# Attention with two key tiles of sixteen as one float, and turning products in the bank of the P V sums

## The chip, the cores and the metric

The kernel runs on one core of a Trainium2 chip. The core has five engines that run their own instruction streams and wait for each other by semaphores: TensorE (PE in the profile; PEld are its weight loads), VectorE (DVE), ScalarE (ACT), GpSimd (POOL) and SyncE (SP), which here only starts DMA transfers. Matrix products land in PSUM, which has eight banks of 128 partitions x 512 floats. The metric is the device time of one execution in microseconds.

## The reference

One transformer block with modulation from a condition vector. The input is 2048 rows of 512 floats. First `h = layernorm(x) * (1 + ca) + sa`, then attention with 32 heads of 16 columns each, and `x + ga * attention(h)`; then a second layernorm with modulation and a mixer block (shifted GELU columns, two more products of 512 x 512, and an MLP of width 1792). The part that the change touches is the attention:

```python
scores = jnp.einsum("bhqd,bhkd->bhqk", q, k) * (Dh ** -0.5)
p = _softmax(scores, axis=-1)
o = jnp.einsum("bhqk,bhkd->bhqd", p, v)
```

All of it is in fp32, and the kernel keeps near-fp32 accuracy by splitting operands into a high and a low part.

## The kernel before

The attention is cut into 64 units: 4 chunks of 512 queries (`ci`) times 16 pairs of heads (`pr`). The two heads of a pair sit in partitions 0 to 63 and 64 to 127. A unit has 16 steps, one for each tile of 128 keys; a step `s` is unit `s // 16`, key tile `s % 16`, and there are 1024 steps.

For each step and head, TensorE makes the transposed scores of 128 keys x 512 queries (`sc`, L1026) and, for a unit 24 steps ahead, a tile of scores the other way round (`mb`, L999), of which VectorE takes the row maximum (`mx`, L995). The maxima of a unit are negated and written by eight small DMAs into extra rows of the query operand (`qtl<-nm`), so that the scores arrive with the maximum subtracted. A score product and a maximum product use the two halves of TensorE's rows and run side by side; the two together are called a row pair here.

ScalarE takes the exponential of `sc` and writes it as a 32-bit integer with 26 binary places into a tile of P (`pt` or `xbs`, L1022), two heads side by side. The upper 16 bits of each integer, read as fp16, are the high part of P. The lower 16 bits must be converted to fp16 first: one instruction of 128 x 1024 elements for each step, on GpSimd (L1075) or, when GpSimd is behind, on ScalarE (L1073, shown as a helper's line L158 in the profile's rows).

P V is then summed in one bank of PSUM (`pv`) by columns. A high column (L1100) is four products of 32 output rows, two per head, and serves one step. A low column (L1097) is again four products and serves two steps. V is stored as three bf16 pieces, a column of a constant that gives the softmax sum, and an fp16 copy for the low column. The four products of a column use four column strips of TensorE.

At a unit's end ScalarE copies the sums (`ac`, L1117), and four fp32 products with a constant matrix turn them and add the three pieces (`ot`, L1127). These are called turning products here. ScalarE copies the result (`sm`, L1134), VectorE takes reciprocals (`rc`, L1142) and GpSimd scales into the output (`osb`, L1138).

The order of all instructions is made by the program itself when it is built. A small planner (`Sched`) keeps a planned time for each engine. The main loop goes through blocks of three row pairs. For each block it emits the row pairs, the conversions of earlier steps and then the P V columns that are due by a list of gates (`pvs`), and the other engines' work follows by planned costs (CROW 232, CCOL 240 ns and so on). Of the eight banks one is the bank of the P V sums, and seven are shared by `sc`, `mb` and all other products (`NSM`). The turning products take one of these seven and are slipped in by a generator (`o_fin`) when a bank and time are free. TensorE, like each engine, works strictly through its own list.

While query chunk 0 runs, the remaining projections of Q, K and V are slipped in between the blocks. After that the attention runs alone, and near its end the first part of the mixer begins (`tail(0)`, 30 steps before the end); the other three parts of the mixer follow after the attention. The weights of the mixer come as 1 MB pieces (`wr<-Ws`). The first three are started 140 steps before the attention's end, with a planned pause of 3 us after each, and then four row blocks of x are loaded from ScalarE's DMA queue (L1295). K and Q of a unit (`kst<-Ks`, `qtl<-Qs`) are loaded two units ahead and V (`vst<-Vs`) six steps ahead, all from SyncE's queue.

P lies in six tiles of a pool and, from step 264 on, in two more that use a buffer of the mixer (`xbs`); a low column is delayed by up to three half steps (`LOWLAG`).

Of the kernel before, what the change touches and what calls it, by code (L numbers as in the profile page):

```python
# [83 lines left out]
XBF = 4  # L84
XBT = 4
T0S = 30
T0L = 140
T0W = 3000.0
RATE3 = 1000.0
BURST3 = 1300.0  # L90
BF, BR = 2, 3
# [14 lines left out]
LNG = (1, 3)  # L106
LNC = 2
VP = 2
WIDE = range(S // CH * 64 + 8, 984)
LOWLAG = 3  # L110
XB = 4


# [219 lines left out]
def kernel(ctx, tc, A_x, A_wqkv, A_wo, B_w1, B_w2, B_w3, B_w4, c, w_mod, out):  # L333
# [93 lines left out]
    def dbank(n):  # L427
        return sch.take(lambda i: psd["d"].tile([P, CH], F32, name=n, tag=f"s{i}" if psd["s"] else f"d{i}", bufs=1))
# [540 lines left out]
            load_rows(kst[u % 3], j, Ks, h, slice(0, S), slice(0, S))  # L969

    def load_v(u):
        vst[u] = at.tile([P, NKT, 192], BF16, name="vst", tag="vst", bufs=2)
        sch.dma(dma.dma_start, vst[u], Vs[units[u][1]])

    sm = Slots(NSM)
    ptx = []
    e_exp, e_hi, e_low, v_free, acs = {}, {}, {}, [0.0], []

    def bank(nm):
# [23 lines left out]
    def new_pt(s):  # L1003
        if s in WIDE:
            i = pn[0] % (NPT + len(ptx)) - NPT
            pn[0] += 1
            if i >= 0:
                pt[s] = ptx[i]
                return
        pt[s] = at.tile([P, 2, CH], I32, name="pt", tag="pt", bufs=NPT)  # L1010

    def score_part(s, j):

        u, kt = divmod(s, NKT)
        if j == 0:
            new_pt(s)
        x, b = bank("sc")
        ready, sm.t[x] = sm.t[x], LATE
        r = slice(64 * j, 64 * j + 64)

        def after(e):
            ea = sch.crit("A", 480, e + PX, lambda: act.activation(pt[s][:, j], b, AF.Exp))  # L1022
            sm.t[x] = ea + XP["A"]
            if j:
                e_exp[s] = e_hi[s] = ea
        return ready, lambda: te.matmul(b, kst[u % 3][r, kt * P:(kt + 1) * P], qst[u][r], start=True, stop=True), after  # L1026

    def row_pair(s, j):
# [33 lines left out]
    def p_low(s):  # L1062
# [11 lines left out]
        else:  # L1074
            e_low[s] = XP["G"] + sch.crit("G", 1345, ready, lambda: pool.tensor_scalar(  # L1075
                o, i, 0.5, 1.0, op0=OP.mult, op1=OP.mult))

    def pv_ready(s, lo):

        return max(e_low[s], e_low[s + 1]) if lo else max(e_hi.pop(s), v_free[0] if s % NKT == 0 else 0.0)  # L1080

    def pv_part(s, lo):
# [27 lines left out]
    def ac_copy():  # L1110
        u, e = acs.pop()
        while u and ("ot", u - 1) not in done:
            sch.step()
        ac = at.tile([P, CH], F32, name="ac", tag="ac", bufs=1)
        vst.pop(u)
        acc = pv.pop(u)
        e = sch.crit("A", cA(), e + PX, lambda: act.activation(ac, acc, AF.Copy))  # L1117
        v_free[0] = e + XP["A"]
        sch.add(o_fin(u, ac, e + XP["A"]), 0)

    def o_fin(u, ac, ready):
        ci, pr = units[u]
        yield lambda: sch.T["P"] >= ready and sch.room()
        n = 2 * (DH + 1)
        b = dbank("ot")[:, :TPC * n]
        for t in range(TPC):
            te.matmul(b[:, t * n:(t + 1) * n], ac[:, t * P:(t + 1) * P], smat.rearrange("p j d -> p (j d)"), start=True, stop=True)  # L1127
            yield 110
        done.add(("ot", u))
        sm = at.tile([P, 8, DH + 1], F32, name="sm", tag="sm", bufs=2)  # L1130
        rc = at.tile([P, 8, 1], F32, name="rc", tag="rc", bufs=2)

        def sums():
            act.activation(sm.rearrange("p th d -> p (th d)"), b, AF.Copy)  # L1134
            sch.free(b)

        def fin():
            pool.tensor_tensor(osb[ci][:, :, pr * 32:pr * 32 + 32].rearrange("p t (h d) -> p t h d", d=DH),  # L1138
                              sm[:, :, 0:DH].rearrange("p (t h) d -> p t h d", h=2),
                              rc.rearrange("p (t h) o -> p t h o", h=2).to_broadcast([P, TPC, 2, DH]), op=OP.mult)  # L1140

        sch.chain(("A", 170, sums), ("D", 90, lambda: dve.reciprocal(rc, sm[:, :, DH:DH + 1])), ("G", 350, fin),  # L1142
                  *([mark(("att", ci))] if pr == NP - 1 else []), prio=0, bank=b)


    GW = 130 + CH + 2
# [141 lines left out]
    def tail_loads():  # L1288
        rings["0"] = Ring(FRONT, [], "r")
        for _ in range(BR):  # L1290
            rings["0"].add([("wr", BR)])
            yield sch.wait(T0W)
        for t in range(TPC):
            x1t[t] = fa.tile([P, D], F32, name="x1", tag="x1", bufs=X1F)
            act.dma_start(x1t[t], x_d[t * P:(t + 1) * P])  # L1295

    def tail(ci):
        end = ci == NC - 1
# [147 lines left out]
        def gelu(b, n, hi, lo, key):  # L1446
            me = gn[0]
            gn[0] += 1
            live.append(me)
            sq = fa.tile([P, 3 * P], F32, name="sq", tag="sq", bufs=XB)[:, :n]  # L1450
# [149 lines left out]
    def before(s):  # L1600
# [17 lines left out]
    blocks = [list(range(i, min(i + GRP, 2 * NS))) for i in range(-2 * LEAD, 2 * NS, GRP)]  # L1618
    pvs = []
    for s in range(0, NS, 2):  # L1620
        low = 2 * s + 2 + (min(LOWLAG, 2 * (NKT - 2 - s % NKT)) if s in WIDE else 0)
        pvs += [(2 * s, s, 0), (2 * s + 2, s + 1, 0), (low, s, 1)]
    pvs.sort(key=lambda x: x[0])
    due = 0.0
    for k, blk in enumerate(blocks + [[]] * (LAG + CPER)):
# [13 lines left out]
        if k >= LAG and (k % CPER == 0 or not blk):  # L1639

            x = (blocks[min(k - LAG, len(blocks) - 1)] or [-1])[-1]
            while pvs and pvs[0][0] < x and not (col and pvs[0][1] % NKT == 0 and not pvs[0][2]):
                col.append(pvs.pop(0)[1:])
        t, start = CIN, 0.0
        need = sum((s >= 0) + (s + LEAD < NS) for s, _ in row)
        sch.flush(need)
# [6 lines left out]
            t += CROW  # L1653
        t += CMID
        for s, i in col:
            start = max(start, pv_ready(s, i) - t)
            t += CCOL
        sch.gap(start)
        sch.flush(need)
        sch.T["P"] = max(sch.T["P"], start) + CIN  # L1660
# [8 lines left out]
            p_low(s)  # L1669
        sch.T["P"] += CMID  # L1670
        for s, i in col:
            pv_part(s, i)
        sch.T["P"] += COUT
        for e in "ADG":
            sch.misc(e, max(sch.T["P"], sch.T[e]) + TOLE[e])
        if s0 < 0:
            sch.fill(LEADB / 2 * len(blk))
        elif sch.gens:
# [5 lines left out]
        if 2 * (NS // NC) - 1 in blk:  # L1684
# [8 lines left out]
            fa = o0x.enter_context(tc.tile_pool(name="fa", bufs=1, side="right"))  # L1693
            big = {"A4": fa.tile([P, 4 * KT * 2 * P], F32R, name="A")}
            xbs = fa.tile([P, XBF, D], F32, name="xbs")
            xns = {k: fa.tile([P, XN[k], D], F32, name=k) for k in ("xn", "xf")}
            xnum = {"xn": 0, "xf": 0}
            ptx += [xbs[:, 2 * i:2 * i + 2].bitcast(I32) for i in range(2)]
            big["A"] = big["A4"]
        if blk and blk[0] <= 2 * (NS - T0L) <= blk[-1]:  # L1700
            sch.add(tail_loads())
        if blk and blk[0] <= 2 * (NS - T0S) <= blk[-1]:
            sch.add(tail(0))
    if acs:
# [53 lines left out]
```

## Time and profile before

| | |
|---|---|
| median of 3 runs | 2003.88 us (2003.48 to 2003.94) |
| profiled execution | 2006.74 us, its span 2004.8 us |
| TensorE, weight loads | 1939.3 us, 1161.6 us busy |
| VectorE | 1656.6 us busy (83%) |
| ScalarE | 1519.9 us busy (76%) |
| GpSimd | 1551.9 us busy (77%) |
| first and last copy of P V sums (L1117) | at 167.8 and 1513.7 us |
| row maxima (L995) | 2048, 678 ns mean |
| exponentials (L1022) | 1688 + 360, 623 and 639 ns mean |
| conversions on GpSimd (L1075) | 773 + 165, 1367 and 1363 ns mean |

The time has three stages: up to about 520 us the projections and query chunk 0, to about 1514 us the rest of the attention, and then the mixer. A row of a group gives the line, engine, operation, output and inputs, shapes, the count, busy microseconds and mean nanoseconds of one, and after the second bar the idle time just before them with what ended it. Mean durations overlap for instructions that follow each other in a pipeline, so the distance between starts tells more than a duration. The first numbers of a timeline row are start and length in microseconds.

### The profile page before, as it was taken

Reading aid. Unit: us, or ns where it says so; the run is one execution under the profiler, and the core shown is the slowest. Engines: PE = TensorE matmul, PEld = TensorE weight load, DVE = VectorE, ACT = ScalarE, POOL = GpSimd, SP = SyncE. Lnnn points to the kernel's source line nnn. Section 1 sums busy time; section 2 is a strip of 40 time slices with the busy share of each in tenths; the row PEclk is TensorE's granted clock in tenths of the full one; section 3 lists DMA queues with packets and bytes.
Section 4 is the critical chain, followed back from the end, with each engine's and each line's share of the span. In section 5 each row is a group of like instructions: output and inputs, shape, how many; then the busy total and the mean of one; then the engine's idle time right before and its main releaser. Section 6 shows DMA issues by size and latency. Waiting matters only on the chain.

```text
span 2004.8 us, 41627 instructions
## 1 busy us (share of the span) xinstructions
PE 1939.3 (97%) x14456; PEld 1161.6 (58%) x14456; DVE 1656.6 (83%) x2979; ACT 1519.9 (76%) x3100; POOL 1551.9 (77%) x1473
## 2 busy tenths in 40 slices
PE   7999999999999999999999999999998899999999
PEld 5755554554444444444444444444456788888998
DVE  6398888879999999999999999998976786656443
ACT  6438987768999999999999999998985545344443
POOL 6339998888999999999999999998995564435222
PEclk9989999999999999999999999999999999999999
DMA  8777665454444444444434343545415666553541
GB/s 292 235 196 190 158 177 175 131 135 124 94 83 97 87 94 90 91 91 90 94 87 95 86 96 85 107 115 128 94 38 213 225 235 266 217 205 112 199 152 69
DMA packets 185507, 277.99 MB, mean 139 GB/s; under 512 B 117105, under 2 KB 127857, under 8 KB 169009
## 3 DMA queue, kind: packets, MB, share of 16 engines
q1 hardware_dynamic: 181792, 267.20, 49.3%
q10 hardware_dynamic: 2304, 4.20, 0.6%
q0 software_dynamic: 1200, 3.93, 0.5%
q8 instruction: 115, 1.88, 0.4%
q14 instruction: 96, 0.78, 0.1%
HBM read 211.81 MB, written 62.91 MB: 137 GB/s over the span
## 4 chain that ended last, share of the span: by engine, by line
PE 61%; DVE 11%; DMA 4%; ACT 4%; POOL 3%; issue 2%; SPq 1%; ACTq 0%; POOLq 0%; DVEq 0%
PE mb L999 15%; PE sc L1026 10%; PE pv L1100 10%; DVE mx L995 8%; PE w L365 5%; PE w L361 5%; PE w L363 5%; PE pv L1097 4%; PE ot L1127 3%; ACT pt L1022 2%; DMA wr<-Ws 2%; POOL pt L1075 1%; PE xT L1261 1%; POOL trs L1370 1%; PE q L365 1%
## 5 line engine op out<-in xcount | busy, mean ns | idle before, releaser
L995 DVE TENSOR_REDUCE mx<-mb 128x1 f32<-128x512 f32 x2048 | 1249.7, 678 | 61.7 <-PE mb L999 54.0
L1075 POOL TENSOR_SCALAR pt<-pt 128x1024 f16<-128x1024 uint16 x773 | 1017.7, 1367 | 73.0 <-ACT pt L1022 72.6
L1022 ACT ACTIVATE pt<-sc 128x512 int32<-128x512 f32 x1688 | 890.3, 623 | 94.7 <-PE mb L999 65.6
L999 PE MATMUL mb<-kst,qtl 62*128 62x512 f32 x2048 | 787.0, 464 | 20.1 <-ACT pt L1022 7.7
L1026 PE MATMUL sc<-qtl,kst 64*128 64x512 f32 x2048 | 745.1, 451 | 3.7 <-DVE mx L995 1.8
L999 PEld LDWEIGHTS mb<-kst,qtl 62*128 62x128 f32 x2048 | 361.9, 193 | 263.3 <-ACT pt L1022 136.6
L1026 PEld LDWEIGHTS sc<-qtl,kst 64*128 64x128 f32 x2048 | 338.2, 185 | 189.2 <-DVE mx L995 116.9
L1100 PE MATMUL pv<-pt,vst 128*32 128x512 f16 x3376 | 318.6, 396 | 4.6 <-ACT ac L1117 4.6
L1479 POOL TENSOR_TENSOR g<-sq,g 128x256 fp32r<-128x256 f32 (+1 forms) x124 | 96.7, 784 | 189.7 <-ACT g L1478 176.0
L1075 POOL TENSOR_SCALAR xbs<-xbs 128x1024 f16<-128x1024 uint16 x165 | 219.6, 1363 | 4.4 <-ACT xbs L1022 4.3
L1022 ACT ACTIVATE xbs<-sc 128x512 int32<-128x512 f32 x360 | 200.0, 639 | 10.9 <-PE mb L999 9.5
L1100 PEld LDWEIGHTS <-vst 128*32 128x32 bf16 x4096 | 91.4, 94 | 182.9 <-issue 164.5
L1097 PE MATMUL pv<-pt,vst 128*32 128x512 f16 (+1 forms) x1688 | 173.0, 392 | 1.3 <-POOL pt L1075 1.3
L363 PE MATMUL w<-A,wr 128*128 128x256 f32 (+1 forms) x520 | 154.2, 297 | 0.3 <-DVE A L351 0.3
L361 PE MATMUL w<-A,wr 128*128 128x256 f32 (+1 forms) x520 | 154.2, 297 | 0.0
L365 PE MATMUL w<-A,wr 128*128 128x256 f32 (+1 forms) x520 | 154.0, 296 | 0.0
L1475 ACT ACTIVATE sq<-w 128x256 f32<-128x256 f32 (+1 forms) x130 | 52.0, 401 | 127.8 <-PE w L365 117.4
L361 PE MATMUL w<-wr,g 128*128 128x512 f32 x270 | 108.6, 402 | 3.0 <-DMA wr<-Ws 3.0
L365 PE MATMUL w<-wr,g 128*128 128x512 f32 x270 | 108.0, 400 | 3.1 <-POOL g L1479 3.1
L363 PE MATMUL w<-wr,g 128*128 128x512 f32 x270 | 107.7, 399 | 0.0
L1457 DVE SCALAR_TENSOR_TENSOR sq<-sq,w 128x256 f32<-128x256 f32 (+1 forms) x130 | 58.1, 449 | 55.6 <-ACT sq L1477 55.5
L363 PEld LDWEIGHTS w<-A,wr 128*128 128x128 f32 x520 | 99.6, 191 | 1.7 <-DVE A L351 0.5
(172 smaller groups left out, 2461.0 us busy)
## 6 DMA issues: line engine op xcount, KB each, us to landing
wr<-Ws SPq DMA_DIRECT2D x66, 1024.0 KB, 5.6
vst<-Vs SPq DMA_DIRECT2D x64, 768.0 KB, 5.2
kst<-Ks SPq DMA_DIRECT2D x126, 384.0 KB, 6.2
Ws<-wr SPq DMA_DIRECT2D x14, 1024.0 KB, 5.1
qtl<-Qs SPq DMA_DIRECT2D x128, 96.0 KB, 4.3
Vs<-vt SPq DMA_DIRECT2D x32, 384.0 KB, 4.3
Ks<-qk SPq DMA_DIRECT2D x16, 512.0 KB, 4.1
Qs<-qk SPq DMA_DIRECT2D x16, 512.0 KB, 3.0
```

The costliest lines, as they stand in the source:

```text
L361: te.matmul(o, lh, rh, start=first, stop=False)
L363: te.matmul(o, lh, rl, start=False, stop=False)
L365: te.matmul(o, ll, rh, start=False, stop=last)
L995: end = sch.crit("D", 605, e + PX, lambda: dve.reduce_max(mxs[u][:, j, g, c:c + 1], b, axis=AX.X))
L999: return ready, lambda: te.matmul(b, lhs, kst[u % 3][r, c * CH:(c + 1) * CH], start=True, stop=True), after
L1022: ea = sch.crit("A", 480, e + PX, lambda: act.activation(pt[s][:, j], b, AF.Exp))
L1026: return ready, lambda: te.matmul(b, kst[u % 3][r, kt * P:(kt + 1) * P], qst[u][r], start=True, stop=True), after
L1075: e_low[s] = XP["G"] + sch.crit("G", 1345, ready, lambda: pool.tensor_scalar(o, i, 0.5, 1.0, op0=OP.mult, op1=OP.mult))
L1097: te.matmul(acc[r:r + n, :], v[:, kt + i, c:c + n].bitcast(F16), pt[s + i].bitcast(F16)[:, j, 0::2], start=False, stop=kt == NKT - 2, skip ...
L1100: te.matmul(acc[r:r + 32, :], v[:, kt, r:r + 32], pt[s].bitcast(F16)[:, j, 1::2], start=kt == 0, stop=False, skip_group_check=True)
L1127: te.matmul(b[:, t * n:(t + 1) * n], ac[:, t * P:(t + 1) * P], smat.rearrange("p j d -> p (j d)"), start=True, stop=True)
L1479: ("G", cG(n), lambda: pool.tensor_tensor(lo, sq, hi, op=OP.subtract)), (None, 0, end), bank=b)
```

## The change

For units 17 to 60, key tiles 4 and 5 of the sixteen are handled as one float. ScalarE writes their exponentials as plain fp32 into fixed buffers, no conversion follows, and P V for them is made by fp32 products: for each of the two steps two column pairs of 256 queries each, a pair being one product of 64 output rows for each head (`pv_full`). V for these two tiles is made into fp32, with its scale, by one GpSimd instruction of 128 x 256 elements per unit. The four column pairs of a unit have gates three half steps apart.

For units 18 to 60 the turning products no longer take one of the seven banks. They are an entry of the list of gates, stand alone in a block and go into the bank of the P V sums, after ScalarE has copied the sums from it; the next unit's first P V column waits until ScalarE has copied the turned result out again.

From step 264 on P has nine tiles instead of eight: six of the pool and three in other buffers of the mixer (`xn`, `xf`, `sqs`). The old `xbs` buffer holds the two steps in fp32. Low columns may be delayed by five half steps, and a block takes at most three P V columns.

The three weight pieces and the four row blocks of x are started one by one behind the V loads of units 55 to 59: a piece each at 55, 56 and 57, two row blocks each at 58 and 59. The buffers `sq` of the mixer become parts of one tile.

The core of the diff:

```diff
-T0L = 140
-T0W = 3000.0
+T0U = (55, 56, 57, 58, 59)
...
+FU = range(17, 61)
+FK = 4
+FGATE = (1, 4, 7, 10)
+CFULL = 460.0
 WIDE = range(S // CH * 64 + 8, 984)
-LOWLAG = 3
+SUMS = range(18, 61)
+LOWLAG = 5
+COLS = 3
+CSUM = 900.0
...
+        if u in FU:
+            sch.chain(("G", 360, lambda: pool.tensor_scalar(vfull[u % 2], v[:, FK:FK + 2, 0:128], 2.0 ** -20, 2.0 ** -20,
+                                                            op0=OP.mult, op1=OP.mult)), prio=0, ready=e)
...
+        if full(s):
+            p = pfull[s % 2][j]
+        else:
+            if j == 0:
+                new_pt(s)
+            p = pt[s][:, j]
...
-            ea = sch.crit("A", 480, e + PX, lambda: act.activation(pt[s][:, j], b, AF.Exp))
+            ea = sch.crit("A", 480, e + PX, lambda: act.activation(p, b, AF.Exp))
...
+    def pv_full(s, n):
+
+        u, kt = divmod(s, NKT)
+        c = slice(256 * n, 256 * n + 256)
+
+        def mms():
+            for j in range(2):
+                r = slice(64 * j, 64 * j + 64)
+                te.matmul(pv[u][r, c], vfull[u % 2][:, kt - FK, r], pfull[s % 2][j][:, c], start=False, stop=False,
+                          skip_group_check=True)
+        sch.put("P", CFULL, 0.0, mms)
...
+    def o_now():
+
+        u, ac = ots.pop()
+        b = ap_.tile([P, CH], F32, name="ot", tag="v", bufs=1)[:, :TPC * 2 * (DH + 1)]
+        e = sch.put("P", CSUM, 0.0, lambda: [o_sums(b, u, ac, t) for t in range(TPC)])
+        done.add(("ot", u))
+        sums, rest = o_rest(u, b)
+        v_free[0] = sch.crit("A", 170, e + PX, sums) + XP["A"]
+        sch.chain(*rest, prio=0, ready=v_free[0])
...
+            if nu in T0U:
+                tail_load(nu - T0U[0])
...
+        if full(s):
+            pvs += [(2 * s + x, s + i // 2, 3 + i % 2) for i, x in enumerate(FGATE)]
+            continue
...
+        if s % NKT == NKT - 2 and s // NKT in SUMS:
+            pvs.append((low, s, 2))
```

Where a fp32 column pair stands on TensorE, just behind the low column of the tiles before it. Before, in the same place of a unit (L1097 is the low column, L1100 a high one; `sc` and `mb` are the products of the row pairs):

```order
L1097 LDWEIGHTS vst
L1097 MATMUL pv<-xbs,vst 32x512
L1026 MATMUL sc<-qtl_145,kst_147 128x512
L999 MATMUL mb<-kst_967,qtl_965 128x512 x2
L1026 MATMUL sc<-qtl_145,kst_147 128x512 x2
L999 MATMUL mb<-kst_967,qtl_965 128x512
L1100 LDWEIGHTS vst
L1100 MATMUL pv<-pt,vst 32x512
```

After (L1106 is a column pair with P from `xbs` and the fp32 V, which lies in `xn`; L1131 is the low column, L1046 and L1011 the row pairs):

```order
L1131 LDWEIGHTS vst
L1131 MATMUL pv<-pt,vst 32x512
L1106 MATMUL pv<-xbs,xn 64x256 x2
L1046 MATMUL sc<-qtl_145,kst_147 128x512
L1011 MATMUL mb<-kst_1105,qtl_1103 128x512 x2
L1046 MATMUL sc<-qtl_145,kst_147 128x512 x2
L1011 MATMUL mb<-kst_1105,qtl_1103 128x512
L1131 LDWEIGHTS vst
L1131 MATMUL pv<-xn,vst 32x512
```

Between a low column and the next three row pairs now stand two fp32 products, one for each head. The other three pairs of a unit stand in the next three blocks.

The turning products on TensorE at a unit's end. Before (`ot`, L1127):

```order
L1100 LDWEIGHTS vst
L1100 MATMUL pv<-pt,vst 32x512
L1127 MATMUL ot<-smat,ac 128x34 x4
L999 MATMUL mb<-kst_967,qtl_965 128x512
L1026 MATMUL sc<-qtl_145,kst_147 128x512 x2
L999 MATMUL mb<-kst_967,qtl_965 128x512 x2
L1026 MATMUL sc<-qtl_145,kst_147 128x512
```

After (L1160):

```order
L1131 LDWEIGHTS vst
L1131 MATMUL pv<-pt,vst 32x512
L1011 MATMUL mb<-kst_967,qtl_965 128x512
L1046 MATMUL sc<-qtl_145,kst_147 128x512 x2
L1011 MATMUL mb<-kst_967,qtl_965 128x512 x2
L1046 MATMUL sc<-qtl_145,kst_147 128x512
L1160 MATMUL ot<-smat,ac 128x34 x4
L1046 MATMUL sc<-qtl_145,kst_147 128x512
```

Before, they followed a P V column of the next unit in the same block; now they follow three row pairs directly, and the next unit's first column comes behind the three row pairs after them.

The weight pieces on SyncE's queue (`Ws_92` and `Ws_82` are the second and third piece). Before:

```order
L137 DMA wr<-Ws_92 128x2048
L137 DMA vst<-Vs 128x3072
L137 DMA qtl_145<-nm 1x128x2 x8
L137 DMA wr<-Ws_82 128x2048
L137 DMA qtl_1103<-Qs 48x512
L137 DMA kst_1105<-Ks 48x2048
```

After:

```order
L143 DMA vst<-Vs 128x3072
L143 DMA wr<-Ws_92 128x2048
L143 DMA qtl_1103<-nm 1x128x2 x8
L143 DMA qtl_965<-Qs 48x512
L143 DMA kst_967<-Ks 48x2048
```

A piece now stands directly behind a V load and ahead of the small shift rows, no longer directly ahead of the loads of Q and K.

More of the change, by code (lines that the diff above doesn't have):

```diff
@@ L971, in load_v, with full @@
     def load_v(u):
-        vst[u] = at.tile([P, NKT, 192], BF16, name="vst", tag="vst", bufs=2)
-        sch.dma(dma.dma_start, vst[u], Vs[units[u][1]])
+        v = vst[u] = at.tile([P, NKT, 192], BF16, name="vst", tag="vst", bufs=2)
+        e = sch.dma(dma.dma_start, v, Vs[units[u][1]])
+        if u in FU:
+            sch.chain(("G", 360, lambda: pool.tensor_scalar(vfull[u % 2], v[:, FK:FK + 2, 0:128], 2.0 ** -20, 2.0 ** -20,
+                                                            op0=OP.mult, op1=OP.mult)), prio=0, ready=e)
+    def full(s):
+        return s // NKT in FU and s % NKT in (FK, FK + 1)
     sm = Slots(NSM)
-    ptx = []
+    ptx, ots, vfull, pfull = [], [], [], []
     e_exp, e_hi, e_low, v_free, acs = {}, {}, {}, [0.0], []
@@ L1286, in cols_mm, with tail_load @@
                 yield nsq(n)
-    def tail_loads():
-        rings["0"] = Ring(FRONT, [], "r")
-        for _ in range(BR):
+    def tail_load(i):
+        if i == 0:
+            rings["0"] = Ring(FRONT, [], "r")
+        if i < BR:
             rings["0"].add([("wr", BR)])
[L1292 to L1295, printed above, removed]
+        else:
+            for t in range(2 * (i - BR), 2 * (i - BR) + 2):
+                x1t[t] = fa.tile([P, D], F32, name="x1", tag="x1", bufs=X1F)
+                act.dma_start(x1t[t], x_d[t * P:(t + 1) * P])
     def tail(ci):
@@ L1449, in gelu @@
             live.append(me)
[L1450 removed]
+            sq = sqs[:, me % XB * 3 * P:][:, :n]
             def end():
@@ L1695 @@
             xbs = fa.tile([P, XBF, D], F32, name="xbs")
+            sqs = fa.tile([P, XB * 3 * P], F32, name="sqs")
             xns = {k: fa.tile([P, XN[k], D], F32, name=k) for k in ("xn", "xf")}
             xnum = {"xn": 0, "xf": 0}
-            ptx += [xbs[:, 2 * i:2 * i + 2].bitcast(I32) for i in range(2)]
+            pfull += [[xbs[:, 2 * i + j] for j in range(2)] for i in range(2)]
+            vfull += [xns["xn"][:, 2, 256 * i:256 * i + 256].rearrange("p (k d) -> p k d", k=2) for i in range(2)]
+            ptx += [x[:, 0:2].bitcast(I32) for x in xns.values()]
+            ptx.append(sqs[:, :2 * CH].rearrange("p (j n) -> p j n", j=2).bitcast(I32))
             big["A"] = big["A4"]
-        if blk and blk[0] <= 2 * (NS - T0L) <= blk[-1]:
-            sch.add(tail_loads())
         if blk and blk[0] <= 2 * (NS - T0S) <= blk[-1]:
```

52 lines of the change are left out of this document (37 added, 15 removed).

## The prediction

> **What bounds the kernel now.** I read the page first, then busy time by stretch, groups and waits in the steady part of the attention, and last the timelines of TensorE and VectorE at places where one waits. The instruction order of the two kernels is the same up to the end of query chunk 0's units and again after the attention, so only units 17 to 60 and the loads near unit 57 can move time. Busy time of each engine by stretch:
>
> ```profile
> core 0: us, PE busy (x) PEld busy (x) DVE busy (x) ACT busy (x) POOL busy (x), PEclk, DMA share, GB/s
> 582.50:1339.60 757.10, 750.64 (x6390) 349.92 (x6392) 743.34 (x1295) 724.68 (x1433) 728.78 (x623) 1.00 0.44 92
> 1339.60:1405.00 65.40, 61.70 (x506) 28.33 (x506) 58.59 (x103) 57.82 (x114) 57.54 (x50) 0.95 0.58 138
> 1405.00:1514.00 109.00, 105.53 (x862) 52.88 (x861) 86.35 (x153) 94.29 (x187) 104.64 (x97) 1.00 0.30 73
> ```
>
> The groups of nearly the same stretch (583 to 1340 us): count, busy us, mean ns, idle before and its releaser.
>
> ```profile
> L995 DVE TENSOR_REDUCE mx<-mb 128x1 f32<-128x512 f32 x1219 | 741.4, 678 | 12.4 <-PE mb L999 8.8 <-PE sc L1026 2.6
> L1075 POOL TENSOR_SCALAR pt<-pt 128x1024 f16<-128x1024 uint16 x408 | 534.6, 1363 | 17.0 <-ACT pt L1022 17.0
> L1075 POOL TENSOR_SCALAR xbs<-xbs 128x1024 f16<-128x1024 uint16 x139 | 184.9, 1363 | 3.8 <-ACT xbs L1022 3.6
> L158 ACT ACTIVATE pt<-pt 128x1024 f16<-128x1024 uint16 x50 | 70.0, 1400 | 0.0
> L999 PEld LDWEIGHTS mb<-kst,qtl 62*128 62x128 f32 x1218 | 217.3, 192 | 161.5 <-ACT pt L1022 91.6 <-DVE mx L995 32.9 <-ACT xbs L1022 23.3
> L1127 PE MATMUL ot<-smat,ac 128*128 128x34 f32 x304 | 41.1, 280 | 0.0
> ```
>
> A unit has 32 maxima, so 1219 of them are 38.1 units and one unit takes 757.1 / 38.1 = 19.87 us. Per unit VectorE is busy 743.3 / 38.1 = 19.51 us, ScalarE 19.02, GpSimd 19.13. VectorE idles only 0.36 us per unit; that caps the gain. Its own pace, from an undisturbed stretch, and two stretches around a wait:
>
> ```profile
> 1398.65 12.59 DVE L995 TENSOR_REDUCE mx<-mb 128x1 f32<-128x512 f32 x21
> ...
> 929.39 6.05 DVE L995 TENSOR_REDUCE mx<-mb 128x1 f32<-128x512 f32 x10
> 935.76 1.89 DVE L995 TENSOR_REDUCE mx<-mb 128x1 f32<-128x512 f32 x3 [0.32 <-PE sc L1026]
> 937.57 0.20 DVE L1142 RECIPROCAL rc<-sm 128x8 f32<-128x8 f32 x1
> ```
>
> From start to start a maximum takes (12.59 - 0.68) / 20 = 0.596 us. 32 of them are 19.06 us; the two small instructions of a unit (0.2 us each, partly overlapped) make about 19.3 us. That is the floor of a unit: 0.57 us below today. TensorE's busy share of 99% says little, since modelled ends overlap; its starts say more:
>
> ```profile
> 931.95 0.41 PE L1100 MATMUL pv<-pt,vst 128*32 128x512 f16 x4
> 932.19 0.41 PE L1097 MATMUL pv<-xbs,vst 128*32 128x512 f16 x4
> 932.41 0.41 PE L1100 MATMUL pv<-pt,vst 128*32 128x512 f16 x4
> 932.75 0.49 PE L1026 MATMUL sc<-qtl,kst 64*128 64x512 f32 x1
> ...
> 933.33 0.39 PE L999 MATMUL mb<-kst,qtl 62*128 62x512 f32 x1
> 933.65 0.41 PE L1100 MATMUL pv<-pt,vst 128*32 128x512 f16 x4
> 933.89 0.39 PE L1097 MATMUL pv<-pt,vst 128*32 128x512 f16 x4
> 934.21 1.08 PE L1127 MATMUL ot<-smat,ac 128*128 128x34 f32 x8
> 935.22 0.50 PE L999 MATMUL mb<-kst,qtl 62*128 62x512 f32 x1
> ```
>
> A block of three row pairs and three P V columns takes 933.65 - 931.95 = 1.70 us when nothing waits; a column more or less is 0.23 us, so a block is 1.01 us plus 0.23 per column, and a change of tile shape costs about 0.09 (0.32 against 0.23). A unit has 10.67 blocks, 24 columns and one set of turning products (934.21 to 935.22, 1.0 us): 10.8 + 5.5 + 1.0 = 17.3 us. TensorE has 2.5 us to spare per unit; VectorE, GpSimd and ScalarE have less than one each.
>
> **The change part by part.**
>
> *Two steps of sixteen as fp32.* In 44 units two steps lose their low half: 88 of 1024 conversions go. By the order of the two kernels GpSimd does 879 instead of 938 and ScalarE 57 instead of 86. 59 x 1.36 = 80 us at most leave GpSimd and 29 x 1.40 = 41 us leave ScalarE. GpSimd gains 44 conversions of V (128x256); the trace has no such instruction, its nearest rows are the quicker and the slower of these, together with the fp32 product's nearest row:
>
> ```profile
> L1138 POOL TENSOR_TENSOR osb<-sm,rc 128x128 f32<-128x128 f32 x64 | 26.0, 407 | 8.7 <-DVE rc L1142 8.5
> L789 POOL TENSOR_TENSOR vt<-vr,vt 128x256 bf16<-128x256 f32 x32 | 22.7, 714 | 36.6 <-ACT vt L788 36.6
> 40.59 1.89 PE L808 MATMUL vb<-wab,gcol 128*128 128x256 f32 x8
> ```
>
> A fourth of L1075's 1.36 us is 0.34, L789 is 0.71: 15 to 31 us, I take 20. Per unit GpSimd falls by about 1.4 us to 17.8, ScalarE by 0.9 to 18.1. Neither is near the pace after that, and this is worth nothing by itself: VectorE's floor of 19.3 stays. It is worth the waits that they cause: TensorE's row loads wait for ScalarE 91.6 + 23.3 us in the stretch, most of it in TensorE's spare time.
>
> TensorE pays. Two high columns and one low column per unit go: 24 columns become 21, -0.69 us. Added are four fp32 column pairs of 256 columns. The 8 records of four full-width fp32 products of that size take (1.89 - 0.38) / 7 = 0.216 us each, two per product: 0.43 us for one product. A pair has two products in the two 64-column halves. Side by side they cost 0.43 us, staggered by a record 0.65, one after the other 0.86; each pair also brings a change of shape or two, 0.1 to 0.18. The fp16 columns above put four products side by side in 0.23 us, so side by side is what the nearest row shows, and I take 0.43 + 0.10 = 0.53. TensorE then needs 10.8 + 21 x 0.23 + 0.9 + 4 x 0.53 = 18.6 us per unit, still under 19.3.
>
> But the four pairs stand in four blocks in a row. At the quoted wait the last maximum's product started at 933.33 and the next at 935.22, 1.89 us apart, and VectorE idled 0.32: it has work for about 1.57 us between these two starts. A block that ends in high, low and fp32 pair needs 0.32 + 0.24 + 0.32 + 0.53 = 1.41, one with a pair between two columns about 1.5. Both pass, but such a block takes 2.0 to 2.1 us where three maxima take 1.79, so the lead is eaten by the second or third. I charge 0.2 us of new VectorE idling per unit (0 to 0.45).
>
> *Turning products in the bank of the P V sums.* They now follow three row pairs with no column ahead: 0.32 + 1.01 = 1.33 us between the two starts, instead of 1.89. So the 0.32 us wait, once per unit, goes. The bank that they took from the seven for scores and maxima stays free, and with the two lighter engines I take half of the other 0.2 us between busy time and floor, 0.1. The price is a second handover through ScalarE in the bank (copy, products, copy, next unit's first column). TensorE waits in order there, with the row pairs of the next block behind it. Before, the single handover cost this:
>
> ```profile
> L1100 PE MATMUL pv<-pt,vst 128*32 128x512 f16 x3376 | 318.6, 396 | 4.6 <-ACT ac L1117 4.6
> ```
>
> That is 4.6 us in all 64 units. Between the two ScalarE copies and their users stands a whole block of rows (0.9 us); I charge nothing, at most 0.3 us per unit.
>
> Nine P tiles instead of eight, the longer delay of the low columns and the cap of three columns per block only cut the long blocks: nothing beside what is counted.
>
> *The early weight loads.* This is the one place with a long stall:
>
> ```profile
> 1353.16 0.59 SPq L137 DMA_DIRECT2D wr<-Ws  x1
> ...
> 1358.73 0.30 SPq L137 DMA_DIRECT2D kst<-Ks  x1
> ...
> 1368.61 0.89 PE L999 MATMUL mb<-kst,qtl 62*128 62x512 f32 x2 [3.49 <-DMA kst<-Ks]
> ...
> 1369.40 1.29 DVE L995 TENSOR_REDUCE mx<-mb 128x1 f32<-128x512 f32 x2 [3.35 <-PE mb L999]
> ```
>
> A 1 MB weight piece and four row loads of x go out just ahead of K for the next unit, and K comes late. The stretch 1339.6 to 1405 has 103 VectorE instructions, 34 per unit, so 3.03 units: 60.2 us at 19.87, and it took 65.4. The change puts each piece right behind a V load, with these medians to land:
>
> ```profile
> wr<-Ws SPq DMA_DIRECT2D x66, 1024.0 KB, 5.6
> vst<-Vs SPq DMA_DIRECT2D x64, 768.0 KB, 5.2
> kst<-Ks SPq DMA_DIRECT2D x126, 384.0 KB, 6.2
> 1339.45 0.34 SPq L137 DMA_DIRECT2D vst<-Vs  x1
> 1354.29 0.42 SPq L137 DMA_DIRECT2D kst<-Ks  x1
> ```
>
> V and piece need 10.8 us and K follows 14.8 us after V, so all 5.2 us come back (at least 3, if the eight small shift rows behind the piece are late once).
>
> *Sum.* Per unit -0.32 + 0.2 - 0.1 = -0.22 us, in 44 units -9.7; the stall -5.2: -14.9. The profiled execution has a span of 2004.8 and 1.9 us around it (2006.74); the median of the runs is 2003.88, 0.14% lower. The same saving from the median gives 1989.
>
> **The rivals.**
>
> *Staggered fp32 pairs: slower.* If the second half's first record can start only when the first half's second one does, a pair costs 0.65 + 0.15 = 0.80 us. TensorE then needs 16.5 + 3.2 = 19.7 us per unit and passes VectorE's floor; the block ends in 0.32 + 0.24 + 0.32 + 0.75 = 1.63 to 1.75 us, above the 1.57, and four blocks in a row are each 0.4 us too long, of which the lead hides about a half. That is 0.8 to 1.2 us of idling against 0.42 saved: +0.4 to +0.8, middle +0.55 per unit, +24 us, less 5.2: 2022. It decides from a pair of about 0.7 us on. For it: each fp32 product is two records, and they are issued one half after the other. Against: the columns in fp16 run four at once. Fully one after the other would be 20.5 us of TensorE and 2045.
> The Trainium skill ("TensorE: Matmul & The Clock Gate", Part 3, The mechanism) says that matmuls start and end in strict program order even across tiles; that rule speaks for this rival. No row of this kernel has two records of one tile ahead of one of another, so the trace neither bears it out nor denies it.
>
> *Only the stall comes back.* The new idling eats the whole wait of the turning products, or the second handover costs 0.2 us per unit: 1998.7, between 1996 and 2007.
>
> *VectorE reaches its floor.* The fp32 pairs are hidden and all 0.57 us go: 44 x 0.57 + 5.2 = 30, 1974; 1974 to 1981.
>
> **How the numbers follow.** Forecast 0.45 (1989, own range 1981 to 1996), floor 0.12, only the stall 0.16, staggered or serial pairs 0.27. The range that leaves out half of the floor's case and most of the staggered one's upper part is 1976 to 2022. About 0.2% (4 us) is what a measurement tells from no change, so faster means under 1999.9: 0.45 + 0.12 + half of 0.16 = 0.65; same 0.09; slower 0.26.
>
> **What would show it.** Right: four fp32 records of a pair within 0.45 us from first start to next instruction's start; units of about 19.65 us; no VectorE wait behind the turning products; no 3 us wait for K. Wrong: the third record of a pair starting 0.2 us after the first and VectorE waiting 0.2 us or more in most fp32 blocks; or TensorE waiting for ScalarE's copies of the sums in most units.

## The result: 1.3% slower

The kernel before took 2003.68 us in the median of its four runs, the changed one 2030.32 us (2027.24 to 2033.15). The ratio is 1.0133, with a 95% interval of 1.0117 to 1.015. The forecast was 1989, with a range of 1976 to 2022. All times here are medians of runs at a granted clock of 0.98 to 0.99; one run of one experiment, 2071.87 us at a clock of 0.85, is left out.

The page of the changed kernel begins like this (span, and busy time of each engine):

```profile
span 2025.5 us, 41832 instructions
## 1 busy us (share of the span) xinstructions
PE 1969.0 (97%) x14632; PEld 1171.2 (58%) x14632; DVE 1662.3 (82%) x2979; ACT 1497.5 (74%) x3071; POOL 1503.9 (74%) x1458
```

GpSimd and ScalarE have less to do, as intended: 48 and 22 us less than before. The time went the other way. The same stretches as in the prediction, of the changed kernel:

```profile
582.50:1339.60 757.10, 755.93 (x6328) 349.85 (x6324) 723.82 (x1251) 681.45 (x1360) 661.55 (x589) 1.00 0.41 89
1339.60:1405.00 65.40, 65.40 (x550) 30.51 (x542) 62.75 (x110) 59.32 (x120) 56.95 (x52) 1.00 0.56 133
```

In the first stretch VectorE does 1251 instructions instead of 1295 and idles 33 us instead of 14. In the second it does 110 instead of 103: the long wait for K is gone.

The row maxima count the units. Here is the group of the maxima between 600 and 1300 us, first in the kernel before, then in the changed one:

```profile
L995 DVE TENSOR_REDUCE mx<-mb 128x1 f32<-128x512 f32 x1127 | 685.4, 678 | 11.6 <-PE mb L999 8.3 <-PE sc L1026 2.4
```

```profile
L1007 DVE TENSOR_REDUCE mx<-mb 128x1 f32<-128x512 f32 x1089 | 664.7, 679 | 22.3 <-PE mb L1011 19.2 <-PE sc L1046 0.6
```

With 32 maxima per unit, a unit takes 700 x 32 / 1127 = 19.88 us before and 20.57 us after. These 0.69 us in 44 units are 30 us, and the wait for K gives 5 to 6 back: that is about the result, 26.6 us.

Where in a unit the 0.69 us lie can be read from the starts of the maxima. When nothing waits, two maxima start 0.598 us apart. The table adds up what lies beyond that, from all maxima between 600 and 1300 us, by what TensorE does between their two products (us per unit; the small reciprocal and the last reduction of a unit are in it, about 0.1 us each: in the changed kernel 0.06 of the 0.66 is that reduction, and the reciprocal stands at the turning products, before it stood in blocks with columns). The last column is an experiment of the next section.

| between two maximum products | before | changed | changed, bf16 pairs |
|---|---|---|---|
| one or two columns | 0.31 | 0.10 | 0.11 |
| three or more columns | 0.10 | 0.30 | 0.08 |
| a pair with one or two columns | - | 0.66 | 0.06 |
| turning products | 0.37 | 0.40 | 0.33 |
| nothing | -0.02 | -0.01 | -0.03 |
| sum | 0.76 | 1.45 | 0.56 |

The waits of blocks with columns alone add up to 0.41 before and 0.40 after. Blocks with an fp32 pair are the new cost, and the wait at the turning products did not go. TensorE in two blocks with a pair (L1106), from the timeline of the changed kernel:

```profile
935.65 0.41 PE L1134 MATMUL pv<-pt,vst 128*32 128x512 f16 x4
...
936.21 0.65 PE L1106 MATMUL pv<-xbs,xn 128*64 128x256 f32 x4
936.79 0.50 PE L1011 MATMUL mb<-kst,qtl 62*128 62x512 f32 x1
...
937.37 0.39 PE L1011 MATMUL mb<-kst,qtl 62*128 62x512 f32 x1
...
937.69 0.41 PE L1131 MATMUL pv<-pt,vst 128*32 128x512 f16 x4
938.02 0.65 PE L1106 MATMUL pv<-xbs,xn 128*64 128x256 f32 x4
938.61 0.41 PE L1134 MATMUL pv<-pt,vst 128*32 128x512 f16 x4
938.94 0.49 PE L1046 MATMUL sc<-qtl,kst 64*128 64x512 f32 x1
```

The four records of a pair take 0.65 us together. Two narrow windows on the first of these pairs show two records in each:

```profile
936.21 0.44 PE L1106 MATMUL pv<-xbs,xn 128*64 128x256 f32 x2
...
936.48 0.39 PE L1106 MATMUL pv<-xbs,xn 128*64 128x256 f32 x2
```

So two records start together, and the other two 0.27 us later. The rows do not name the half of a record, but records of one product start 0.216 us apart in the prediction's row of full-width products, so the two that start together belong to different halves: the halves run side by side. From the start of a pair to the next instruction are 0.58 to 0.59 us. From the last maximum product of one block (937.37) to the first row product of the next (938.94) are 1.57 us. VectorE in the same blocks:

```profile
937.36 1.87 DVE L1007 TENSOR_REDUCE mx<-mb 128x1 f32<-128x512 f32 x3
939.51 3.69 DVE L1007 TENSOR_REDUCE mx<-mb 128x1 f32<-128x512 f32 x6 [0.28 <-PE mb L1011]
943.50 1.29 DVE L1007 TENSOR_REDUCE mx<-mb 128x1 f32<-128x512 f32 x2 [0.30 <-PE mb L1011]
```

It waits 0.28 and 0.30 us behind two of the unit's four blocks with a pair. At a unit's end two rows of the waits between 600 and 1300 us matter (total us, times, longest):

```profile
PEld ot L1160 <- ACT ac L1151: 12.0, 34, 1.5
DVE rc L1196 <- ACT sm L1188: 6.3, 23, 1.2
```

In every unit TensorE waits, 0.35 us on average, until ScalarE has copied the sums, before it can start the turning products. In two of three units VectorE's reciprocal then waits for ScalarE's second copy, 0.19 us per unit on average, with the maxima queued behind it.

### The profile page after: what moved, and what is told of

Its sections match the earlier page's. It is cut to its first block, busy times and chain, and to the rows that moved or that the text cites. A ratio compares the mean times of both kernels' runs of the same rounds, so it can differ in the third digit from the quotient of the medians.

```text
span 2025.5 us, 41832 instructions
## 1 busy us (share of the span) xinstructions
PE 1969.0 (97%) x14632; PEld 1171.2 (58%) x14632; DVE 1662.3 (82%) x2979; ACT 1497.5 (74%) x3071; POOL 1503.9 (74%) x1458
## 4 chain that ended last, share of the span: by engine, by line
PE 76%; DVE 9%; ACT 4%; POOL 3%; DMA 3%; issue 3%; SPq 1%; ACTq 0%; POOLq 0%; DVEq 0%
PE mb L1011 17%; PE sc L1046 14%; PE pv L1134 12%; PE pv L1131 5%; PE pv L1106 5%; PE w L371 5%; PE w L367 5%; PE w L369 5%; DVE mx L1007 4%; PE ot L1160 3%; ACT pt L1040 2%; POOL pt L1095 1%; SPq L143 1%; DMA wr<-Ws 1%; DMA wst<-in_A_wqkv_dram 1%
## 5 line engine op out<-in xcount | busy, mean ns | idle before, releaser
L1095 POOL TENSOR_SCALAR pt<-pt 128x1024 f16<-128x1024 uint16 x683 | 904.7, 1368 | 97.0 <-ACT pt L1040 93.6
L1040 ACT ACTIVATE pt<-sc 128x512 int32<-128x512 f32 x1452 | 765.8, 614 | 128.0 <-PE mb L1011 101.0
L1011 PE MATMUL mb<-kst,qtl 62*128 62x512 f32 x2048 | 754.0, 455 | 9.4 <-ACT pt L1040 3.1
L1046 PE MATMUL sc<-qtl,kst 64*128 64x512 f32 x2048 | 722.1, 444 | 2.8 <-DVE mx L1007 1.9
L1011 PEld LDWEIGHTS mb<-kst,qtl 62*128 62x128 f32 x2048 | 353.8, 193 | 218.6 <-ACT pt L1040 99.3
L1046 PEld LDWEIGHTS sc<-qtl,kst 64*128 64x128 f32 x2048 | 337.5, 185 | 162.4 <-DVE mx L1007 85.3
L1134 PE MATMUL pv<-pt,vst 128*32 128x512 f16 x2904 | 271.6, 396 | 4.6 <-ACT ac L1151 4.6
L1534 POOL TENSOR_TENSOR g<-sqs,g 128x256 fp32r<-128x256 f32 (+1 forms) x124 | 97.0, 787 | 188.8 <-ACT g L1533 176.5
L1131 PE MATMUL pv<-pt,vst 128*32 128x512 f16 (+1 forms) x1452 | 163.4, 392 | 1.3 <-POOL pt L1095 1.3
L1530 ACT ACTIVATE sqs<-w 128x256 f32<-128x256 f32 (+1 forms) x130 | 52.1, 401 | 127.2 <-PE w L371 114.4
L1106 PE MATMUL pv<-xbs,xn 128*64 128x256 f32 x704 | 114.8, 405 | 0.0
L1512 DVE SCALAR_TENSOR_TENSOR sqs<-sqs,w 128x256 f32<-128x256 f32 (+1 forms) x130 | 58.1, 449 | 55.4 <-ACT sqs L1532 55.3
L369 PEld LDWEIGHTS w<-A,wr 128*128 128x128 f32 x520 | 98.8, 190 | 1.7 <-DVE A L357 0.5
L367 PEld LDWEIGHTS w<-A,wr 128*128 128x128 f32 x520 | 98.8, 190 | 1.2 <-ACT A L361 0.2
```

Source lines behind the costliest of these rows:

```text
L367: te.matmul(o, lh, rh, start=first, stop=False)
L369: te.matmul(o, lh, rl, start=False, stop=False)
L1011: return ready, lambda: te.matmul(b, lhs, kst[u % 3][r, c * CH:(c + 1) * CH], start=True, stop=True), after
L1040: ea = sch.crit("A", 480, e + PX, lambda: act.activation(p, b, AF.Exp))
L1106: te.matmul(pv[u][r, c], vfull[u % 2][:, kt - FK, r], pfull[s % 2][j][:, c], start=False, stop=False, skip_group_check=True)
L1131: te.matmul(acc[r:r + n, :], v[:, kt + i, c:c + n].bitcast(F16), pt[s + i].bitcast(F16)[:, j, 0::2], start=False, stop=kt == NKT - 2, skip ...
```

## The experiments

All times are medians; the kernel before, run beside them on the same chips, had medians of 2000.2 to 2003.8.

### The early loads alone

```diff
-T0L = 140
-T0W = 3000.0
+T0U = (55, 56, 57, 58, 59)
...
+            if nu in T0U:
+                tail_load(nu - T0U[0])
```

> The kernel before with only the early loads moved behind the V loads of units 55 to 59. The theory that the stall in unit 57 (26.0 us against 19.9 between two copies of sums) is the late K alone: 2003.7 falls by 5 to 6 us to about 1998. The rival that the transfers collide in any place: the stall moves to another unit and the time stays within 2 us of 2003.7.

Measured: 1996.96, before 2002.81 beside it; ratio 0.9966 (0.9951 to 0.998). The stall was the late K alone, and the early loads return 5.8 us. In the changed kernel a piece now goes out 14 us ahead of K:

```profile
1342.19 0.34 SPq L143 DMA_DIRECT2D vst<-Vs  x1
1342.57 0.43 SPq L143 DMA_DIRECT2D wr<-Ws  x1
...
1356.92 0.42 SPq L143 DMA_DIRECT2D kst<-Ks  x1
```

### The fp32 steps taken away

```diff
-FU = range(17, 61)
+FU = range(0)
```

> The changed kernel without the fp32 steps: all sixteen steps are converted again, everything else of the change stays. Theory A (TensorE's time for the fp32 pairs in four blocks in a row starves VectorE; starts of row maxima show 0.66 us per unit beyond 0.598 us behind blocks with a pair): the unit falls from 20.59 to about 19.9, the time from 2030 to about 2001. Theory B (the second handover in the bank of the sums): stays above 2020. Theory C (longer delay and cap of three columns): stays above 2020.

Measured: 2019.17, ratio 1.008 (1.0057 to 1.0102). It lies between the theories. Without the pairs the change is 11 us faster, but still 22 us slower than the early loads alone. So the fp32 steps are not all of it, and something that the prediction had at nothing costs some 20 us.

### The turning products back in one of the seven banks

```diff
-SUMS = range(18, 61)
+SUMS = range(0)
```

> The changed kernel with the turning products back in one of the seven banks; fp32 steps, delay and cap stay. Theory A: within 6 us of 2030, since the pairs stay. Theory B (the handover costs 0.28 to 0.4 us per unit): 2012 to 2018.

Measured: 2059.08, ratio 1.0276 (1.0253 to 1.0298). Neither theory had this: beside the pairs, the bank of the sums is worth 29 us. By the starts of the maxima 0.85 us per unit stand at the turning products now, instead of 0.40. Where a pair and the turning products fall into one block, VectorE loses 1.0 us behind it, in a third of the units.

### The pairs in bf16

The two steps keep their place, buffers and conversions, but P is rounded to bf16 in them, so accuracy of these two steps is given up. The pair then is one record per head and streams once.

```diff
-            pfull += [[xbs[:, 2 * i + j] for j in range(2)] for i in range(2)]
+            pfull += [[xbs[:, 2 * i + j].bitcast(BF16)[:, 0:CH] for j in range(2)] for i in range(2)]
```

(and the same view for V, whose bf16 pieces stay as they are)

> The changed kernel with P and V of the two fp32 steps rounded to bf16, so that the same pairs stream once and not four times (accuracy of these two steps is given up; order, handovers, conversions and buffers stay). Theory A: a pair falls from 0.59 to about 0.25 us from its start to the next instruction, blocks with a pair fall below VectorE's 1.79 us per three maxima, and the time falls to 2000 to 2005. Theories B and C: within 6 us of 2030.

Measured: 1990.7, ratio 0.9935 (0.9911 to 0.9959), faster than theory A's own range. A pair in its timeline:

```profile
944.68 0.30 PE L1106 MATMUL pv<-xbs,xn 128*64 128x256 bf16 x2
944.91 0.49 PE L1046 MATMUL sc<-qtl,kst 64*128 64x512 f32 x1
```

And the group of its maxima between 600 and 1300 us:

```profile
L1007 DVE TENSOR_REDUCE mx<-mb 128x1 f32<-128x512 f32 x1139 | 687.6, 677 | 1.9 <-PE sc L1046 0.8 <-PE mb L1011 0.7
```

From a pair's start to the next instruction are 0.23 us instead of 0.58. VectorE's waits before maxima fall from 22.3 to 1.9 us, and a unit takes 700 x 32 / 1139 = 19.67 us. Each engine goes through its instructions in the order of the changed kernel. So what the fp32 pairs cost on TensorE is what made it slow: 39.6 us, 0.9 us per unit, for 4 x 0.35 = 1.4 us of TensorE's time. What is left over is close to VectorE's pace.

### The pairs issued twice

V is halved in its conversion, and each pair runs twice.

```diff
-        sch.put("P", CFULL, 0.0, mms)
+        sch.put("P", CFULL, 0.0, lambda: [mms() for _ in range(2)])
```

> The changed kernel with each fp32 pair issued twice and V halved for it, so that the sums stay the same and TensorE streams four more pairs per unit at 0.43 us each, 1.7 us. Theory A1 (TensorE's time in these blocks passes through nearly whole, as bf16 pairs gave back 0.9 us per unit): +1.5 to +1.8 us per unit, 2095 to 2110. Rival A2 (the pairs cost by their changes of shape and weight loads, and streaming is hidden): under +0.5 us per unit, below 2052.

Measured: 2102.73, ratio 1.05 (1.0483 to 1.0517). Each unit grows by (2102.7 - 2030.3) / 44 = 1.65 us for the 1.73 us that TensorE streams more. The group of the maxima between 600 and 1300 us:

```profile
L1007 DVE TENSOR_REDUCE mx<-mb 128x1 f32<-128x512 f32 x1010 | 619.8, 681 | 66.6 <-PE mb L1011 63.6 <-PE sc L1046 2.8
```

From a doubled pair's start to the next instruction are 1.01 us. Theory A1 holds: in these blocks what TensorE streams more passes through nearly whole, although TensorE has time to spare elsewhere in the unit. VectorE waits for the maximum products of the next block (63.6 us).

### Two pairs in a block

```diff
-FGATE = (1, 4, 7, 10)
+FGATE = (1, 1, 7, 7)
```

> The changed kernel with the four pairs in two blocks by gates (1, 1, 7, 7) instead of one each in four blocks. If what matters is how far one block passes the 1.57 us that VectorE can bridge, two pairs in a block cost more: 2035 to 2050. If it is the sum over blocks in a row that eats the lead, a light block between them gives it back: 2010 to 2025.

Measured: 2038.67, ratio 1.0178 (1.0163 to 1.0194). Slower than one pair in each of four blocks. By the starts of the maxima the blocks with pairs cost 0.59 us per unit now (0.66 with one pair each), but 0.88 us stand at the turning products instead of 0.40. So a light block between them does not give the time back, and part of the cost moved to the unit's end, where the reciprocal waits 0.66 us per unit for ScalarE's second copy. Why that copy comes later here was not taken apart.

### The small parts alone

Three kernels without fp32 steps and with early loads. The turning products in the bank of the sums, with the old delay and no cap (LOWLAG 3, COLS 99):

> The changed kernel without fp32 steps and with the old delay and no cap of columns (LOWLAG 3, COLS 99): the turning products in the bank of the sums, nine P tiles and early loads stay. If the bank's handover is what makes the kernel without fp32 steps 22 us slower than the early loads alone (VectorE's reciprocal waits for ScalarE's copy 10.0 us in 30 units there, TensorE for its other copy 10.7): 2012 to 2025. If the delay and cap do it: 1995 to 2002.

Measured: 2006.97, ratio 1.0014 (1.0002 to 1.0027).

The new delay and cap, with the turning products in one of the seven banks:

> The changed kernel without fp32 steps and with the turning products in one of the seven banks: delay 5, cap of three columns, nine P tiles and early loads stay. If the handover is the cause: 1994 to 2002, near the early loads alone. If the delay and cap are: 2012 to 2025.

Measured: 2027.57, ratio 1.0122 (1.0102 to 1.0143). Neither kernel fell where one of its two theories had put it: both parts cost something, and the delay and cap most. They were then taken apart:

> Only the nine P tiles in their new buffers and the early loads: no fp32 steps, turning products in one of the seven banks, delay 3, no cap. If the tiles cost nothing, as the prediction had it: within 3 us of the early loads alone (1997), and the 10 us of the kernel with the turning products in the bank beside them (2007) belong to the bank. If they are the cause: 2004 to 2010.

> Nine P tiles, early loads and delay 5 without a cap; no fp32 steps, turning products in one of the seven banks. Delay and cap together gave 2028. If the delay is the cause: 2020 to 2030. If the cap is: 1996 to 2004.

> Nine P tiles, early loads and the cap of three columns with the old delay 3; no fp32 steps, turning products in one of the seven banks. If the cap is the cause of 2028: 2018 to 2030. If the delay is: 1996 to 2004.

Measured: the tiles alone 1998.3 (ratio 0.9988, 0.9977 to 0.9999), the delay with the tiles 2034.04 (1.0165, 1.0145 to 1.0185), the cap with the tiles 2013.59 (1.0064, 1.0042 to 1.0087). The nine tiles cost nothing: between 600 and 1300 us that kernel has 1127 maxima, as many as the kernel before and as the early loads alone. The longer delay alone costs 36 us and the cap alone 15. With the delay, VectorE waits like this:

```profile
931.63 5.47 DVE L1007 TENSOR_REDUCE mx<-mb 128x1 f32<-128x512 f32 x9 [0.67 <-PE mb L1011]
937.55 3.81 DVE L1007 TENSOR_REDUCE mx<-mb 128x1 f32<-128x512 f32 x6 [0.45 <-PE mb L1011]
...
943.79 0.20 DVE L1196 RECIPROCAL rc<-sm 128x8 f32<-128x8 f32 x1 [0.54 <-ACT sm L1188]
```

By the starts of the maxima a unit loses 1.59 us instead of 0.76 with the tiles alone. Of these 0.83 us, 0.57 stand in blocks with columns alone (0.97 instead of 0.40) and 0.24 at the turning products (0.61 instead of 0.37): a third of the units has three columns and the turning products in one block, with 0.77 us lost behind it. A low column that comes later frees two P tiles later and brings the unit's last columns, the copy of the sums and the turning products closer together. Which of these makes the waits was not taken apart.

### The same parts beside the pairs

The changed kernel with the old delay and no cap:

```diff
-LOWLAG = 5
-COLS = 3
+LOWLAG = 3
+COLS = 99
```

> The changed kernel with the old delay (3) and no cap; pairs, turning products in the bank, nine P tiles and early loads stay. Without pairs the new delay and cap cost 12 us beside the bank and about 31 us without it. If they cost the same with pairs: about 2018. If they serve the pairs (a block with a pair is kept to three columns): 2030 or slower, up to 2045.

Measured: 2029.99, ratio 1.0135 (1.0119 to 1.015): no difference to the change as it is. That is a balance and not nothing: by the starts of the maxima the blocks with a pair cost 0.51 us per unit instead of 0.66 and blocks with columns alone 0.29 instead of 0.40, but the turning products cost 0.66 instead of 0.40. Only the fp32 steps, with old delay, no cap and the turning products in one of the seven banks:

> Only the fp32 steps of the change, with nine P tiles and early loads: turning products in one of the seven banks, delay 3, no cap. If a pair costs the same wherever it stands (0.9 us per unit against a bf16 pair, of which the lighter GpSimd and ScalarE give back 0.3 at most): 2022 to 2037. If the handover in the bank is what makes room for the pairs: 2045 to 2060, as with the new delay and cap (2059).

Measured: 2055.01, ratio 1.0254 (1.0222 to 1.0286). And the bf16 pairs with old delay and no cap:

> The kernel with bf16 pairs (accuracy of two steps of sixteen given up) with the old delay and no cap. If delay and cap cost by themselves: 1978 to 1986. If they matter only where blocks run into TensorE's limit, which bf16 pairs do not: within 4 us of 1991.

Measured: 2004.36, ratio 1.0013 (1.0001 to 1.0024): against both theories, delay and cap are worth 14 us to the bf16 pairs. Without them a unit loses 0.83 us instead of 0.56, and 0.20 of that is at the turning products (0.53 instead of 0.33). Together the runs make this table, all with nine tiles and early loads:

| | delay 3, no cap | delay 5, cap 3 |
|---|---|---|
| no pairs, one of the seven banks | 1998.3 | 2027.6 |
| no pairs, bank of the sums | 2007.0 | 2019.2 |
| fp32 pairs, one of the seven banks | 2055.0 | 2059.1 |
| fp32 pairs, bank of the sums | 2030.0 | 2030.3 |
| bf16 pairs, bank of the sums | 2004.4 | 1990.7 |

The parts do not add. The bank of the sums costs 9 us without pairs and saves 25 to 29 with fp32 pairs. Delay and cap cost 29 us, 12, next to nothing (4 and 0), or save 14.

### The reciprocal later

The bf16 kernel with the reciprocal planned 0.9 us later:

```diff
-        sch.chain(*rest, prio=0, ready=v_free[0])
+        sch.chain(*rest, prio=0, ready=v_free[0] + 900.0)
```

> The kernel with bf16 pairs, with the planner told that the turned sums are ready 0.9 us later for the reciprocal alone, so that VectorE meets the reciprocal behind more maxima. VectorE waits there for ScalarE's copy 3.3 us in 600 us with bf16 pairs. If that wait is lost time: 1984 to 1988. If the next block hides it: within 3 us of 1991.

Measured: 1991.91, ratio 0.9938 (0.9918 to 0.9958): no difference. In its trace the turning products cost 0.13 us per unit instead of 0.33, but blocks with three columns 0.19 instead of 0.08; the 0.10 us per unit that remain would be 4 us, less than the runs of one kernel differ (1988 to 1996 with bf16 pairs). So most of that wait was not lost time, and the runs cannot tell the rest from nothing.

With the new delay and cap, the bf16 kernels (1991 and 1992) beat both kernels of the case, at the price of accuracy in two steps of sixteen. With the accuracy kept, the early loads alone are the fastest (1997, or 1998 with the nine tiles).

## Why the prediction was wrong

The prediction's sum was -0.22 us per unit, and the starts of the maxima show +0.69. Three terms make the 0.91 us between them: the pairs 0.46 (0.66 instead of 0.20), the turning products 0.35 (+0.03 instead of -0.32), and the 0.10 that the lighter engines and the free bank were to return and that do not show. In 44 units that is 40 us, which is what lies between 1989 and 2030.

**The largest term that failed is the new idling behind the pairs.** The prediction charged 0.2 us per unit, between 0 and 0.45. The table of starts shows 0.66 (0.60 without the small reduction), and bf16 pairs give back 0.9 in all. The mechanism was named (a block with a pair takes longer than three maxima, and the lead is eaten); its size was off for three reasons. A pair takes 0.58 us to the next instruction and not 0.53, which makes a block with a pair between two columns 1.57 to 1.60 us long between the two products, not "about 1.5".

The 1.57 us that VectorE was said to bridge were read from an idle time of 0.32 us behind 1.89; but maxima that follow each other overlap by some 0.08 us, and the starts tell more: the last of the ten maxima before that wait starts at 934.77 (929.39 + 6.05, less its own 0.67), the next at 935.76. They are 0.99 apart, 0.39 more than VectorE's pace, so it had work for only 1.50. And even that needs a lead. When it is spent, all of a block beyond about 1.2 us is lost: three maxima take 1.79 us, and the other two of a block's products start within 0.58 us. In units whose first block with a pair was 1.36 us long, the second, of 1.58, cost nothing; where the first was 1.49 or longer, the second cost 0.26 to 0.40. In the order of the four blocks the mean loss was 0.06 (that is the reduction), 0.21, 0.13 and 0.26 us, at mean lengths of 1.46, 1.58, 1.35 and 1.51. Blocks of 1.24 to 1.36 lost nothing. TensorE's sum over a unit (18.6 us predicted) was no help, because what VectorE has idled does not come back in later blocks: its pace is its floor.

**The wait at the turning products did not go.** The prediction had -0.32 us per unit from a shorter way between two products (1.33 us). The shortest way is 1.33, but the mean is 1.47: TensorE waits 0.35 us per unit for the copy of the sums, and part of that lengthens the way. In the changed kernel no maximum waits for TensorE at this place any more; instead the reciprocal waits 0.2 us per unit for the second copy, and the reciprocal itself (about 0.1) stands there too. So the cost is 0.40 us against 0.37. Both copies belong to the handover that was charged at nothing because a block of rows stands in between. What the bank gives is room beside the pairs, 25 to 29 us, and that was not foreseen.

**Delay and cap were not free.** "Nothing beside what is counted" was wrong for each alone (36 and 15 us), though the change as it is takes the same time without them.

**Right** were the early loads (5.2 us predicted, 5.8 measured); the nine tiles at nothing; the counts of conversions that leave GpSimd and ScalarE, though their busy time fell by 48 and 22 us and not by about 60 and 41; and side by side as the way in which a pair runs. That the lighter engines are worth nothing by themselves was not run alone. The conversion of V, bounded at 0.34 to 0.71 us, takes 0.41:

```profile
L981 POOL TENSOR_SCALAR xn<-vst 128x256 f32<-128x256 bf16 x29 | 11.8, 407 | 2.3
```

**The slower rival** had the right side, 2022, and the right place, but not the right reason. It needed staggered pairs, 0.8 us each, and was to decide from 0.7 us on; the pairs are side by side and it decided at 0.58. If the second half's first record had to wait for the first half's second one, no two records would start together and the last would start 0.43 us after the first; the rows show two together and the last at 0.27. So the rule of strict order that the Trainium skill ("TensorE: Matmul & The Clock Gate", Part 3, The mechanism) states did not stagger these pairs.

Of the signs of being wrong, the third record at 0.2 us could not tell the rivals apart: side by side, too, the third record starts one record later (0.27). A wait of VectorE of 0.2 us or more stood behind 37 of 136 blocks with a pair, not behind most. TensorE's wait for ScalarE's copies did come in every unit.

For delay and cap beside bf16 pairs (14 us saved) and beside none (29 us lost with one of the seven banks) the traces show in which blocks the time goes, but not why it turns from a loss to a saving; that stays open.

## What to carry to other kernels

When one engine is within 2 or 3% of its own pace, cost a change by the length of each stretch between two deliveries to that engine, not by another engine's sum over the loop. Read from the trace how long it can bridge, with a full lead and with a spent one, and read it from starts, since idle times are shorter than what is lost: here TensorE had over 2 us to spare per unit, and 1.4 us more in four neighbouring blocks still cost 0.9. Parts of a schedule (a bank, a delay, a cap) must be run together as well as alone, since here the sign of two of them turned with the third.

## What the runs showed of the hardware that was not expected

Two fp32 products of 128x256 into the two 64-column halves of TensorE run side by side: their records start two and two, 0.27 us apart, and 0.58 us pass to the next instruction, against 0.43 us for one full-width product. In bf16 the same pair is two records with 0.23 us to the next instruction, as much as a column of four fp16 products.
